# Another order for the first loads of a fused attention and two-layer gated network

## The chip, the core and the metric

The kernel runs on one core of a Trainium2 chip. The metric is device time in microseconds (us) for one execution of the whole program, as the median of several runs on one chip. The engines are named as the profile names them: PE (TensorE, matmul), PEld (its weight load), DVE (VectorE), ACT (ScalarE), POOL (GpSimd) and SP (SyncE, which here issues all the loads and stores).

## The reference

Windowed causal attention with a linear bias by distance, over 4 batches, 8 heads, 576 positions and 64 dimensions, feeds two feed-forward layers over 2304 tokens of width 512. All data are float32.

```python
scores = q @ k.T / sqrt(D) + bias            # window of 128 positions, causal
attn = softmax(scores);  x = attn @ v        # x: 2304 x 512
x = (silu(x @ w_gate) * (x @ w_val)) @ moe_w_out       # d_ff 1536
h = x @ moe2_w_in
y = (h * tanh(softplus(h))) @ moe2_w_out               # d_ff 2048
```

## The kernel before, in words

The weights come in as 64-bit floats, so each block of 1 MB is loaded raw and converted on the core into 32-bit numbers, and these are split into a high and a low half for the products. Converting one block takes one ACT instruction (line 420), five on DVE (lines 435, 440, 425, 428 and 446), and then one ACT instruction (line 121, the high half) and one on DVE (line 124, the low half).

The tokens are cut into five chunks (512, 384, 512, 512 and 384). The attention of the first chunk stands alone at the start of the kernel. After it, the first layer of chunk c is interleaved on PE with the attention of chunk c+1; the second layer comes last. In the first chunk the eight heads go in four pairs. The loads of pair r are called q_r, k_r and v_r here: q and k are one load of 256 KB each and hold both heads of the pair, v is four loads of 64 KB. A head passes through S (scores on PE, line 114; mask and row minimum on DVE, lines 221, 228 and 235; exponential on ACT, line 239; norm on DVE, lines 247 and 250, then on ACT and POOL, lines 254 and 256), T (transposes on PE, line 261; copy on ACT, line 267; two masks on POOL, lines 270 and 274) and, for each pair, O (product with v on PE, then the halves of xt on ACT and DVE, lines 121 and 124). `split` (line 185) scales the q of a pair once on ACT before its first scores.

The order of the first loads is written out in `first()`: for each pair its q, k and v, with weight block w0 (tile wst) after the third pair. After the first score piece come o0, the first block of the output weights (tile wraw), then w1, w2 and w3. The raw blocks share a pool of 12 buffers with the four pairs' tiles and the converted blocks. `conv_w1` and `conv_ring` put the steps of a conversion into a list `bg`, and a loop over the attention's 28 pieces (score, transpose and output pieces of the first chunk) takes steps from it at a rate set by `conv_a` and `conv_b`.

Only PE keeps the order in which the program is written. On the other engines, and on the queue of SP, a planner settles the order when the kernel is built, from the dependencies, the order of the program and its own estimates of cost. At run time each engine takes its instructions in that fixed order, and an instruction that waits holds up all that stand behind it.

Of the kernel before, what the change touches and what calls it, by code (L numbers as in the profile page):

```python
# [18 lines left out]
B, H, S, D = 4, 8, 576, 64  # L19
# [11 lines left out]

SLOT = {1: 0, 2: 1, 3: 2, 5: 3, 6: 4, 7: 5, 4: 6}
CFG = dict(
    order="SSOT", delay0=2, early=[4], pbufs=10, pump_g=2, pump_p=2, lag=4, lastlag=6, evprio=500,
    conv_a=0.1, conv_b=0.9,
)


# [54 lines left out]
def body(ctx: ExitStack, tc: tile.TileContext, qT, kT, vP, w1, w1o, w2, cst, yT):  # L93
# [41 lines left out]
    def attention(ap, p, ci, s_native, upfront):  # L135
# [5 lines left out]
        def s_full(h):  # L141
            return h // 2 < s_native

        def load(h):
            pr, e = divmod(h, 2)
            if s_full(h) and e:
                return
            if upfront:
                t = wp.tile([128, 2048], F32, tag="w", name="qkv")
                q, k = t[:, :p.n], t[:, 512:512 + p.nk]  # L150
                raw["v", pr] = t[:, 1152:1152 + 128 * len(p.kb)].rearrange("p (k d) -> p k d", d=128)
            elif s_full(h):
                q = ap.tile([128, p.n], F32, tag=("qraw", "Q")[pr % 2], name="q32")
                k = ap.tile([128, p.nk], F32, tag=("K1", "KL")[pr % 2], name="k32")
            else:
                q = ap.tile([128, p.n], F32, tag="qraw", name="qraw")
                k = ap.tile([128, p.nk], F32, tag="kraw", name="kraw")
            for s in p.segs:
                cq, ck = slice(s.c0, s.c0 + s.n), slice(s.koff, s.koff + s.kn0 + s.n)
                sq, sk = slice(s.s0, s.s0 + s.n), slice(s.s0 - s.kn0, s.s0 + s.n)  # L160
                if s_full(h):
                    nc.sync.dma_start(out=q[:, cq], in_=qT[s.b, h:h + 2, :, sq].rearrange("h d s -> (h d) s"))
                    nc.sync.dma_start(out=k[:, ck], in_=kT[s.b, h:h + 2, :, sk].rearrange("h d s -> (h d) s"))
                    continue
                for e in range(2):
                    nc.sync.dma_start(out=q[64 * e:64 * e + 64, cq], in_=qT[s.b, h, :, sq])
                    nc.sync.dma_start(out=k[64 * e:64 * e + 64, ck], in_=kT[s.b, h, :, sk])
            raw[h] = (q, k)
            if upfront:
                load_v(pr)  # L170

        def load_v(pr):
            if ("v", pr) not in raw:
                raw["v", pr] = ap.tile([128, len(p.kb), 128], F32, tag=f"v{pr % 2}", name="v")
            v = raw["v", pr]
            for x in p.kb:
                for r in range(128 // x.n):
                    nc.sync.dma_start(out=v[r * x.n:(r + 1) * x.n, x.vi, :], in_=vP[x.b, pr, x.k0:x.k0 + x.n, :])
# [122 lines left out]
    early = {}  # L301

    def attention_pieces(atts):

        heads = [(a, h) for a in atts for h in range(H)]
        pairs = [(a, r) for a in atts for r in range(HP)]
        n = len(heads)
        out = []

        def run(k, f):  # L310
            a, h = heads[k]
            return getattr(a, f)(h)

        def load(k):
            if not heads[k][0].upfront:
                run(k, "load")

        def load_v(r):
            if not pairs[r][0].upfront:
                pairs[r][0].load_v(pairs[r][1])  # L320

        def first():
            if atts[0].upfront:
                for h in range(0, H, 2):
                    run(h, "load")
                    for f in early.pop(h, []):
                        f()
            load(0)
            load_v(0)
            run(0, "split")  # L330
            load(1)
            load_v(1)

        def s_piece(k, g):
            a, h = heads[k]

            def f():
                if k == 0 and g == 0:
                    first()
                a.score(h, g)  # L340
                if g == a.ns - 1:
                    a.norm(h)
                    if k + 1 < n:
                        run(k + 1, "split")
                        if k + 2 < n:
                            load(k + 2)

            return (a.ci, 1.7 if a.s_full(h) else 0.87, f)

        def o_piece(k):  # L350
            a, h = heads[k]

            def f():
                if a.ci not in x_t:
                    x_t[a.ci] = xp.tile([128, 2, CT, 512], F32R, tag="x", name="xt")
                a.outp(h // 2)
                r = a.ci * HP + h // 2 + 2
                if r < len(pairs):
                    load_v(r)

            return (a.ci, a.nk * 0.46, f)

        def t_piece(k):
            a, h = heads[k]
            return (a.ci, 0.48, lambda: a.transp(h))

        def delay(k):
            return CFG["delay0"] if heads[k][0].ci == 0 else 1

        for st in range(n + 4):  # L370
            todo = {"S": [], "T": [], "O": []}
            if st < n:
                todo["S"] = [s_piece(st, g) for g in range(heads[st][0].ns)]
            for k in range(max(0, st - 4), min(st, n)):
                if k + delay(k) == st:
                    todo["T"].append(t_piece(k))
                if k + delay(k) + 1 == st and heads[k][1] % 2 == 1:
                    todo["O"].append(o_piece(k))
            for c in CFG["order"]:
                if todo[c]:  # L380
                    out.append(todo[c].pop(0))
            for c in "SOT":
                out += todo[c]
        out.sort(key=lambda x: x[0] > 0)
        return out
# [8 lines left out]
    def pump(n):  # L394
        while n > 0 and bg:
            k, f = bg.popleft()
            f()
            n -= 1
            if k is not None:
                done.add(k)  # L400
# [70 lines left out]
    def stage_w1(i):  # L471
        stage[i] = wp.tile([128, 2048], I32, tag="w", name="wst")
        nc.sync.dma_start(out=stage[i], in_=w1[i].bitcast(I32))

    def stage_other(key, src):
        stage[key] = bpool["a"].tile([128, 2048], I32, tag="wraw", name="wraw", bufs=1)
        nc.sync.dma_start(out=stage[key], in_=src.bitcast(I32))

    def conv_w1(i):
        st = {}  # L480

        def put(w):
            wt[i] = w
            stage.pop(i)
            if i + 4 < NF1:
                stage_w1(i + 4)

        steps(("w", i), convert(stage[i], st) + halves(st, w_tile, put))

    def conv_ring(r):  # L490
        st = {}

        def spill_it():
            nc.sync.dma_start(out=w1od[r], in_=st["w"])

        def put(w):
            ring[0, r] = w
            stage.pop(("o", r))
            if r + 1 < NF1 // 2:
                stage_other(("o", r + 1), w1o[r + 1])  # L500

        steps(
            ("ring", 0, r),
            convert(stage["o", r], st) + [spill_it] + halves(st, ring_tile, put),
        )
# [411 lines left out]
    with tc.manual_schedule(engines={mybir.EngineType.PE}):  # L917
# [18 lines left out]
        atts = [attention(app, p, ci, S_FULL[ci], ci == 0) for ci, p in enumerate(plansA)]  # L936
# [1 line left out]
        lasts = [max(j for j, x in enumerate(pieces) if x[0] == ci) + 1 for ci in range(len(plansA))]  # L938
        at = 0
        stages = [lambda: stage_w1(0), lambda: stage_other(("o", 0), w1o[0]), lambda: stage_w1(1)]  # L940
        for h, k in zip(CFG["early"], range(3)):
            early.setdefault(h, []).append(stages[k])
        stages = stages[len(CFG["early"]):]
        while at < lasts[0]:
            pieces.popleft()[2]()
            at += 1
            if at == 1:
                for f in stages:
                    f()
                conv_w1(0)  # L950
                conv_ring(0)
                conv_w1(1)
                nst = len(bg)
                stage_w1(2)
                stage_w1(3)
            f = (at / lasts[0] - CFG["conv_a"]) / (CFG["conv_b"] - CFG["conv_a"])
            while bg and nst - len(bg) < f * nst:
                pump(1)
        carry = []
        for ci, p in enumerate(plansA):  # L960
# [11 lines left out]
            if 1 <= ci < last:  # L972
                k = last - 1
                for i in range((ci - 1) * NF2 // k, ci * NF2 // k):
                    conv_w2(i)
            lag = CFG["lastlag"] if ci == last else 1
# [36 lines left out]
        for f in carry:  # L1013
# [5 lines left out]
        load = nc.scalar.add_instruction(  # L1019
            mybir.InstLoadActFuncSet(name=nc.get_next_instruction_name(), act_func_set_id=25)  # L1020
        )
# [62 lines left out]
```

## Time and profile before

| | |
|---|---|
| median of 3 runs | 969.74 us (969.54 to 971.17) |
| the profiled execution | 970.98 us, of which span 968.9 us |
| PE busy | 929.1 us (96%) |
| PEld busy | 829.6 us (86%) |
| DVE busy | 718.1 us (74%) |
| ACT busy | 526.9 us (54%) |
| POOL busy | 218.8 us (23%) |
| loads and stores | 174.86 MB, mean 180 GB/s |

The span is the time from the first to the last instruction, and all times in the trace count from its start. Busy shares are means over the whole span: the stretch that the change touches is the first 64 us, in which the shares are others than these.

### The profile page before, as it was taken

Reading aid. Unit: us, or ns where it says so; the run is one execution under the profiler, and the core shown is the slowest. Engines: PE = TensorE matmul, PEld = TensorE weight load, DVE = VectorE, ACT = ScalarE, POOL = GpSimd, SP = SyncE. Lnnn points to the kernel's source line nnn. Section 1 sums busy time; section 2 is a strip of 40 time slices with the busy share of each in tenths; the row PEclk is TensorE's granted clock in tenths of the full one; section 3 lists DMA queues with packets and bytes.
Section 4 is the critical chain, followed back from the end, with each engine's and each line's share of the span. In section 5 each row is a group of like instructions: output and inputs, shape, how many; then the busy total and the mean of one; then the engine's idle time right before and its main releaser. Section 6 shows DMA issues by size and latency. Waiting matters only on the chain. (4 is left out here: it accounts for less than half of the span.)

```text
span 968.9 us, 14644 instructions
## 1 busy us (share of the span) xinstructions
PE 929.1 (96%) x5040; PEld 829.6 (86%) x5040; DVE 718.1 (74%) x1359; ACT 526.9 (54%) x1135; POOL 218.8 (23%) x348
## 2 busy tenths in 40 slices
PE   7789999999999999999998998899999999999998
PEld 5447777898998888887877998889999999999997
DVE  5999999788768865478534768778886788777673
ACT  6856667666666664455433445455544645454442
POOL 2531234211110322001014233552012320122000
PEclk9889999999999999999999999999999999999999
DMA  8763334476546743176306993624784257830385
GB/s 285 261 252 143 119 133 148 139 236 220 170 130 195 249 130 115 31 243 216 118 1 221 387 329 106 232 83 145 256 298 148 66 173 251 312 114 21 96 264 183
DMA packets 76921, 174.86 MB, mean 180 GB/s; under 512 B 9136, under 2 KB 52528, under 8 KB 67120
## 3 DMA queue, kind: packets, MB, share of 16 engines
q1 hardware_dynamic: 76848, 173.94, 54.1%
q8 instruction: 40, 0.66, 0.3%
q14 instruction: 33, 0.27, 0.1%
HBM read 138.25 MB, written 35.65 MB: 179 GB/s over the span
## 5 line engine op out<-in xcount | busy, mean ns | idle before, releaser
L114 PE MATMUL g_ps<-xt,w 128*128 128x512 f32 (+1 forms) x1440 | 316.3, 373 | 1.2 <-DVE xt L124 1.2
L114 PEld LDWEIGHTS g_ps<-xt,w 128*128 128x128 f32 x1440 | 258.1, 188 | 37.7 <-issue 2.0
L114 PE MATMUL bk<-xs,win 128*128 128x384 f32 x1008 | 179.0, 336 | 8.1 <-DVE G L684 6.0
L114 PEld LDWEIGHTS bk<-xs,win 128*128 128x128 f32 x1008 | 174.4, 188 | 12.2 <-DVE G L684 9.7
L114 PE MATMUL bk<-op,wout 128*128 128x384 f32 x1008 | 175.8, 334 | 0.8 <-DMA wout<-w2o 0.7
L114 PEld LDWEIGHTS bk<-op,wout 128*128 128x128 f32 x1008 | 174.8, 188 | 1.4 <-issue 1.4
L114 PE MATMUL acc<-hh,ring 128*128 128x512 f32 (+1 forms) x480 | 148.9, 373 | 1.6 <-DVE ring L124 1.5
L121 ACT ACTIVATE op<-G 128x768 fp32r<-128x768 f32 x84 | 70.7, 846 | 66.0 <-PE bk L114 63.4
L114 PEld LDWEIGHTS acc<-hh,ring 128*128 128x128 f32 x480 | 89.0, 188 | 14.9 <-DVE ring L124 2.3
L124 DVE TENSOR_TENSOR op<-G,op 128x768 fp32r<-128x768 f32 x84 | 80.2, 962 | 27.2 <-ACT op L121 26.7
L270 POOL TENSOR_SCALAR_AFFINE_SELECT PT<-PT 128x256 f32<-128x256 f32 (+4 forms) x80 | 42.6, 546 | 253.4 <-ACT PT L267 253.2
L780 POOL TENSOR_TENSOR t<-w 128x256 f32<-128x256 f32 x48 | 44.4, 945 | 224.3 <-DVE win L124 207.7
L114 PE MATMUL acc<-hl,ring 128*128 128x512 f32 (+1 forms) x240 | 88.5, 369 | 1.7 <-DVE hl L124 1.7
L239 ACT ACTIVATE Pt<-Pt,sm 128x128 f32<-128x128 f32 (+1 forms) x160 | 62.5, 392 | 21.5 <-DVE sm L235 21.2
L619 DVE SCALAR_TENSOR_TENSOR t<-t,g_ps 128x512 f32<-128x512 f32 (+1 forms) x60 | 37.6, 627 | 37.4 <-ACT t L618 37.2
L684 DVE TENSOR_TENSOR G<-u,bk 128x384 f32<-128x384 f32 x72 | 38.9, 552 | 31.3 <-PE bk L114 29.2
L1028 ACT ACTIVATE G<-G 128x384 f32<-128x384 f32 x72 | 36.9, 520 | 44.2 <-DVE G L684 44.2
L618 ACT ACTIVATE t<-g_ps 128x512 f32<-128x512 f32 (+1 forms) x60 | 32.8, 547 | 50.3 <-PE g_ps L114 50.2
L627 DVE SCALAR_TENSOR_TENSOR t<-t,g_ps 128x512 f32<-128x512 f32 (+1 forms) x60 | 37.8, 631 | 27.1 <-PE g_ps L114 26.4
L121 ACT ACTIVATE hh<-t 128x512 fp32r<-128x512 f32 (+1 forms) x60 | 35.0, 583 | 41.4 <-DVE t L627 41.4
L254 ACT ACTIVATE Pt<-Pt,sm 128x128 f32<-128x128 f32 (+1 forms) x144 | 46.3, 390 | 12.9 <-DVE sm L250 12.8
L274 POOL TENSOR_SCALAR_AFFINE_SELECT PT<-PT 128x256 f32<-128x256 f32 (+4 forms) x80 | 52.9, 678 | 1.6
(79 smaller groups left out, 1282.2 us busy)
## 6 DMA issues: line engine op xcount, KB each, us to landing
wout<-w2o SPq DMA_DIRECT2D x42, 1024.0 KB, 5.6
wraw<-w SPq DMA_DIRECT2D x16, 1024.0 KB, 5.3
w2o<-chl SPq DMA_DIRECT2D x16, 896.0 KB, 8.6
wst<-w SPq DMA_DIRECT2D x12, 1024.0 KB, 7.2
cw<-w1od SPq DMA_DIRECT2D x24, 512.0 KB, 4.0
w<-w2d SPq DMA_DIRECT2D x24, 512.0 KB, 3.4
w2d<-cw SPq DMA_DIRECT2D x16, 512.0 KB, 4.0
wraw<-w1o SPq DMA_DIRECT2D x6, 1024.0 KB, 6.4
```

Of the source, the lines that this page charges most:

```text
L114: nc.tensor.matmul(out=out, lhsT=lhsT, rhs=rhs, start=start, stop=stop, skip_group_check=True)
L121: return nc.scalar.activation(out=out, in_=in_, func=AF.Copy)
L124: return nc.vector.tensor_tensor(out=out, in0=in_, in1=hi.bitcast(F32), op=ALU.subtract)
L239: nc.scalar.activation(out=Pt[:q.qn], in_=Pt[:q.qn], func=AF.Exp, scale=-1.0, bias=sm[:q.qn, i:i + 1], accum_out=sm[:q.qn, 8 + i:9 + i],)
L254: nc.scalar.activation(out=pt, in_=pt, func=AF.Copy, scale=r)
L270: nc.gpsimd.affine_select(out=here, in_=prev, pattern=[[0, m], [1, n]], compare_op=ALU.is_ge, fill=0.0, base=0, channel_multiplier=-1,)
L274: nc.gpsimd.affine_select(out=prev, in_=prev, pattern=[[0, m], [-1, n]], compare_op=ALU.is_gt, fill=0.0, base=0, channel_multiplier=1,)
L619: nc.vector.scalar_tensor_tensor(out=t[:, :n], in0=t[:, :n], scalar=1.0, in1=st["g"][:, :n], op0=ALU.add, op1=ALU.mult)
L627: nc.vector.scalar_tensor_tensor(out=t[:, :n], in0=t[:, :n], scalar=0.5, in1=vps[:, :n], op0=ALU.mult, op1=ALU.mult)
L684: nc.vector.tensor_tensor(out=out, in0=a, in1=b, op=op)
L780: nc.gpsimd.tensor_tensor(out=x[:, o], in0=a, in1=b, op=ALU.subtract)
L1028: nc.scalar.activation(out=out, in_=in_, func=AF.Mish)
```

## The change

The order of the first loads becomes a list, in which q stands for a pair's q and k, v for its values, and w0, w1, w2 for the three first stages (block w0, then o0, then block w1). `load` no longer loads the values itself. All three stages are now issued in `first()`, and `conv_a` falls from 0.1 to 0.0: the first step of a conversion is offered after the first piece of the attention (before: after the third); the last of the 22 steps is offered after piece 26 in both.

Order before: q0 k0 v0, q1 k1 v1, q2 k2 v2, w0, q3 k3 v3, o0, w1, w2, w3. Order after: q0 k0, w0, q1 k1, v0, q2 k2, o0, v1, q3 k3, v2, w1, v3, w2, w3.

```diff
-    order="SSOT", delay0=2, early=[4], pbufs=10, pump_g=2, pump_p=2, lag=4, lastlag=6, evprio=500,
-    conv_a=0.1, conv_b=0.9,
+    order="SSOT", delay0=2, early=["q0", "w0", "q1", "v0", "q2", "w1", "v1", "q3", "v2", "w2", "v3"], pbufs=10, pump_g=2, pump_p=2, lag=4, lastlag=6, evprio=500,
+    conv_a=0.0, conv_b=0.9,
...
             raw[h] = (q, k)
-            if upfront:
-                load_v(pr)
...
             if atts[0].upfront:
-                for h in range(0, H, 2):
-                    run(h, "load")
-                    for f in early.pop(h, []):
-                        f()
+                for c, i in ((x[0], int(x[1])) for x in CFG["early"]):
+                    {"q": lambda: run(2 * i, "load"), "v": lambda: atts[0].load_v(i), "w": lambda: early[i]()}[c]()
...
         stages = [lambda: stage_w1(0), lambda: stage_other(("o", 0), w1o[0]), lambda: stage_w1(1)]
-        for h, k in zip(CFG["early"], range(3)):
-            early.setdefault(h, []).append(stages[k])
-        stages = stages[len(CFG["early"]):]
+        early.update(enumerate(stages))
...
             if at == 1:
-                for f in stages:
-                    f()
                 conv_w1(0)
                 conv_ring(0)
                 conv_w1(1)
```

## Rows read from the trace of the kernel before

**Rows 1.** Busy time by stretch: busy us of each engine, PE clock, DMA share, GB/s.
```profile
8.33:17.14 8.81, 8.81 (x31) 7.14 (x31) 5.27 (x34) 6.77 (x26) 1.65 (x6) 1.00 0.95 306
17.14:29.80 12.66, 10.42 (x35) 5.95 (x33) 12.62 (x31) 10.10 (x26) 6.12 (x7) 1.00 0.99 370
...
43.06:64.15 21.09, 13.07 (x51) 6.90 (x51) 19.01 (x36) 14.31 (x30) 9.25 (x13) 0.76 0.89 327
64.15:129.35 65.20, 63.81 (x295) 47.36 (x295) 59.98 (x133) 39.91 (x99) 12.69 (x22) 1.00 0.37 129
```

**Rows 2.** Waits of PE, 6 to 64.2: us, times, longest.
```profile
PE o_ps L114 <- POOL PT L274: 6.6, 5, 3.0
...
PE t_ps L261 <- POOL Pt L256: 1.4, 3, 1.0
```

**Rows 3.** Timeline of PE: start us, duration us; idle time before it in brackets.
```profile
6.22 7.10 PE L114 MATMUL s_ps<-qkv 64*128 64x256 f32 x24 [6.22 <-ACT qkv L185]
...
64.15 0.72 PE L114 MATMUL g_ps<-xt,w 128*128 128x512 f32 x2 [1.24 <-DVE xt L124]
```

**Rows 4.** Waits of DVE, 8.33 to 17.3: us, times, longest.
```profile
DVE sm L247 <- ACT Pt L239: 2.1, 2, 1.3
DVE cw L435 <- DMA wst<-w: 0.9, 1, 0.9
```

**Rows 5.** Timeline of the queue of SP: start of an issue, its duration.
```profile
4.08 0.43 SPq L162 DMA_DIRECT2D qkv<-qT  x1
...
8.48 1.91 SPq L178 DMA_DIRECT2D qkv<-vP  x4
10.43 0.43 SPq L473 DMA_DIRECT2D wst<-w  x1
10.90 0.43 SPq L162 DMA_DIRECT2D qkv<-qT  x1
...
14.33 0.65 SPq L477 DMA_DIRECT2D wraw<-w1o  x1
17.14 1.67 SPq L473 DMA_DIRECT2D wst<-w  x3
```

**Rows 6.** Loads of rows 5, in their order from q1, us from issue to landing.
```profile
qkv<-qT SPq DMA_DIRECT2D x1, 256.0 KB, 4.4
...
wst<-w SPq DMA_DIRECT2D x1, 1024.0 KB, 6.7
qkv<-qT SPq DMA_DIRECT2D x1, 256.0 KB, 6.9
...
wraw<-w1o SPq DMA_DIRECT2D x1, 1024.0 KB, 7.9
...
wst<-w SPq DMA_DIRECT2D x1, 1024.0 KB, 7.6
```

**Rows 7.** Timeline of DVE: the six instructions that convert block w0.
```profile
17.14 0.69 DVE L435 TENSOR_SCALAR cw<-wst 128x1024 int32<-128x1024 int32 x1 [0.87 <-DMA wst<-w]
17.87 1.23 DVE L440 SCALAR_TENSOR_TENSOR cw<-wst,cw 128x1024 f32<-128x1024 uint32 x1
...
19.01 0.42 DVE L425 TENSOR_SCALAR cp<-cg 128x512 int32<-128x512 int32 x1
...
19.86 0.68 DVE L428 SCALAR_TENSOR_TENSOR cp<-cg,cp 128x512 int32<-128x512 int32 x1
...
21.14 1.31 DVE L446 SCALAR_TENSOR_TENSOR cw<-cw,cp 128x1024 f32<-128x1024 f32 x1
...
26.36 1.21 DVE L124 TENSOR_TENSOR w<-cw,w 128x1024 fp32r<-128x1024 f32 x1
```

**Rows 8.** Timeline of ACT: q1's scale, head 0's first exponential, w0's first step.
```profile
8.48 0.72 ACT L185 ACTIVATE qkv<-qkv,cst_sb 128x512 f32<-128x512 f32 x1 [2.31 <-DMA qkv<-qT]
9.19 0.40 ACT L239 ACTIVATE Pt<-Pt,sm 128x128 f32<-128x128 f32 x1
...
17.14 1.16 ACT L420 ACTIVATE cg<-wst 128x1024 bf16<-128x1024 bf16 x1 [0.64 <-DMA wst<-w]
```

## The prediction

> **What bounds the kernel now.** I read the busy time by stretches first, because the change touches only the start. From 64.15 us on PE is the bound: of the 65.20 us up to 129.35 it is busy 63.81 [rows 1]. So whatever moves the moment at which PE gets the last part of the first chunk's xt moves the end, as long as DVE keeps up; DVE is busy 59.98 of the same 65.20 us and has 5.2 us to spare. That moment is 64.15 us, where PE goes on after 1.24 us of waiting for the low half of xt from DVE [rows 3].
>
> Then I asked what sets the 64 us. The waits of PE between 6 and 64 us name POOL: 6.6 us for the masks of PT, 1.4 us for the norm on POOL [rows 2]. But POOL has work for only 9.25 of the last 21.09 us of that phase, so it is not its own load that sets the time [rows 1]. The stretches show who is full: between 17.14 and 29.80 us DVE is busy 12.62 of 12.66 us, and between 43.06 and 64.15 us 19.01 of 21.09 [rows 1]. In both stretches DVE alternates between attention and the conversion of weights. The reader is to see the contrast with the stretch before: from 8.33 us (its first score) to 17.14 us DVE is busy 5.27 of 8.81 us, so 3.54 us lie idle [rows 1]. It waits there 2.1 us for exponentials and, at the end, 0.9 us for block w0 to land [rows 4]. At 17.14 us w0 lands, and its conversion begins on ACT and DVE in the same instant [rows 7, 8].
>
> **How the loads queue.** The first of v2 is issued at 8.48 us, which is when q1 lands (4.08 plus 4.4), and w1 is issued at 17.14 us, when w0 lands (10.43 plus 6.7) [rows 5, 6]. Between the members of each couple stand seven other loads. So in this program a load is issued only when the one eight places before it has landed. With that and about 0.47 us for an issue (10.43 to 10.90) [rows 5] the new order can be counted through.
>
> **The change, part by part.** *w0 goes forward.* It is the fourth load; four issues before q1's old place (4.08) give about 2.2 us. With its own 6.7 us it lands at 8.9 us. The row had a longer queue ahead of it, so that may be late; with the slowest load of a block among these, 7.9 us [rows 6], it is 10.1. So it comes about 8 us earlier, into the stretch in which DVE has idle time. Its six DVE instructions are 0.69 + 1.23 + 0.42 + 0.68 + 1.31 + 1.21 = 5.54 us [rows 7]. The idle time is 3.54 us. Lower bound of the gain: only the wait for w0 itself goes, 0.9 us [rows 4]. Upper bound: all 3.54 us are filled. I take two thirds, 2.4 us: the pieces are about as long as the longest gap (1.3 us) [rows 4], so a piece put into a gap will often stick out and delay an instruction of the attention, but there are several gaps and w0 is there before most of them.
>
> *ACT.* Two instructions of w0 move with it, 1.16 us [rows 8] and a high half that I take as the same. ACT is idle 8.81 - 6.77 = 2.04 us in that stretch [rows 1], so they just fit: 0, and up to 1.2 us lost if one of them stands before exponentials that are due.
>
> *q1 and k1 go behind w0.* q3 was issued directly behind w0 and took 6.9 us, against q1's 4.4 [rows 6]. Issued at 2.67 us, q1 lands at 9.57 instead of 8.48, and its scale of 0.72 us [rows 8] ends at 10.3. PE needs it for the third of three heads, whose 24 matmuls take 7.10 us from 6.22 [rows 3]: two thirds of it end at 10.95. So PE still has work for 0.6 us and this costs 0. Without that cover it costs the 1.1 us by which q1 is later.
>
> The Trainium skill speaks against this edit: by "DMA: Bandwidth & Descriptors", section "Queues, rings and completion order", each DMA engine consumes descriptors in the order of its ring, so that q1 would wait for the whole of w0. At the 306 GB/s of the stretch [rows 1] the 1.05 MB of w0 are 3.4 us instead of the 2.5 us by which q3 was slower; q1's scale would end at 11.2, PE would wait 0.3 us, and the sum below would be -2.1 instead of -2.4. No run here shows the rings themselves.
>
> *Values go back.* v0 is issued from 3.6 to 5.5 us and so lands by about 10; O comes after the scores of three heads, whose matmuls end at 13.3 us [rows 3], and v1 is needed two heads later still. Nothing waits: 0.
>
> *o0, w1, w2, w3.* k2 must wait for w0 (8.9), o0 for q1 (9.57). o0 lands at 9.57 + 7.9 = 17.5 instead of 22.2. The second load of v2 stands eight places behind o0 and so waits until 17.5; w1, three issues later, goes at about 18.9, 1.8 us later than now, and w2 and w3 with it. w1 lands then at 26.5 instead of 24.7 us. DVE has o0 to convert until then, as full as it is from 17.14 to 29.80 [rows 1], so 0; if it ran dry, up to 1.8 us. The next chunk's loads behind these move by as much; PE reads them only after 64 us.
>
> *First steps offered at once.* The steps are offered two pieces earlier, but none can run before w0 lands at 8.9 us. 0 by itself; it lets the planner use the gaps that the first term counts.
>
> **Sum.** -2.4 + 0 + 0 + 0 = -2.4 us. The profiled execution took 970.98 us (span 968.9 and 2.1 around it), so 968.6; that execution was 1.24 us above the median of the runs, so against the median it is 967.3 us. About 0.2%, or 1.9 us, can be told from no change. Bounds of the first term alone: 966.2 to 968.8.
>
> **The rivals.** *Given back.* DVE is full from 17.14 us on because the planner fills it with conversions that PE does not need yet. If w0 leaves this stretch, later blocks may take its place, and the chain through POOL at 43 to 64 us stays as long as it is. For it: PE idles 8.0 of 21.09 us there [rows 1], and POOL's masks are its longest wait [rows 2]. Against it: later blocks can't come earlier than their loads, and w1 to w3 land later, not earlier. Time 969.7.
>
> *More than that.* The granted PE clock in 43.06 to 64.15 us is a mean of 0.76 [rows 1], a mix of 2.4 and 1.2 GHz, in a stretch in which PE is idle for 8.0 us. If the waits go, PE's 13.07 us become 9.9 at full clock: up to 3.1 us more. For it: after 64.15 us, where PE hardly idles, the mean is 1.00 [rows 1]. Against it: the waits of this stretch are not removed by the change itself. Time 964.2.
>
> *Slower: ACT is held up at the start.* The scale of q1 stands ahead of head 0's first exponential on ACT now, and waited 2.31 us for its load [rows 8]. If the planner keeps it there and puts w0's first step ahead of both, ACT stands until w0 has landed. With a landing at 10.1 us: 1.16 to 11.3, 0.72 to 12.0, and the exponentials begin at 12.0 instead of 9.19. Every head follows: +2.8 us, and DVE, which waits for the exponentials, has the same idle time as before. Time 972.5. It decides from a landing of about 9.7 us on, where the delay exceeds what DVE gains. For it: the planner's estimate was too early each time here (2.31 us at q1, 0.64 us at w0 [rows 8]). Against it: with q1 behind 1 MB its own estimate moves too.
>
> **How the numbers follow.** The gain by filling idle time has 0.46, of which 0.08 lies under 1.9 us; more than that 0.08; given back 0.28; slower 0.18, of which 0.01 is too small to be told. Faster: 0.38 + 0.08 = 0.46. Same: 0.08 + 0.28 + 0.01 = 0.37. Slower: 0.17. The range reaches from the clock's case to near the held-up ACT: 964.0 to 971.8. The likeliest case by itself holds 966.2 to 968.8.
>
> **What the profile after would show.** Right: the first step on wst near 9 us, DVE busy over 7 us between 8.3 and 17.1, the issue of w1 near 19 us, q1's scale from about 9.6 us, and the row where PE goes on after the last xt at about 61.8 us. Wrong: head 0's first exponential later than 10 us on ACT (held up); that last row at 64 us in spite of the early w0 (given back); or an unlike order of the conversions on DVE further on, which would move PE's waits after 64 us by amounts that none of the terms contains.

## The result and the profile after

The changed kernel takes 975.58 us (974.8 to 978.77, 5 runs) against 969.74 us before (967.27 to 971.93, 5 runs). The ratio is 1.0069, 95% interval 1.0047 to 1.0092: slower by 0.7%, or 5.8 us between the medians. The profiled execution took 974.84 us, its span 972.9 us against 968.9, so a comparison of the two traces has to explain 4.0 us. Line numbers in the conversions and the attention are 2 to 4 lower than before.

The stretches that answer to [rows 1]; the columns are the same.

```profile
8.33:17.14 8.81, 7.92 (x26) 6.33 (x25) 7.60 (x30) 5.91 (x20) 0.88 (x3) 1.00 1.02 358
17.14:29.80 12.66, 10.46 (x31) 6.84 (x31) 12.66 (x35) 10.29 (x30) 7.93 (x11) 1.00 0.98 360
29.80:43.06 13.26, 12.34 (x64) 8.44 (x60) 12.10 (x45) 11.45 (x35) 6.31 (x13) 1.00 0.71 231
43.06:64.15 21.09, 12.11 (x46) 6.16 (x47) 19.03 (x32) 13.35 (x29) 11.75 (x14) 0.61 0.82 299
64.15:129.35 65.20, 64.75 (x297) 48.06 (x296) 59.99 (x127) 38.14 (x91) 9.98 (x22) 1.00 0.40 137
```

DVE (third of the engines) is busy 7.60 us where it was busy 5.27: the hole is filled, as foretold. But in the next stretch it is as full as it was, 12.66 of 12.66 us, and between 43.06 and 64.15 us it is busy 19.03 us where it was 19.01. Nothing has been taken out of the later stretches. For the stretch from 29.80 us, which [rows 1] leaves out, the kernel before has:

```profile
29.80:43.06 13.26, 12.55 (x53) 8.49 (x52) 11.83 (x40) 10.80 (x31) 10.97 (x15) 0.74 0.65 220
```

What the loads did, in the queue of SP (start of an issue, its duration), answering to [rows 5]:

```profile
2.18 0.43 SPq L469 DMA_DIRECT2D wst<-w  x1
2.65 0.43 SPq L162 DMA_DIRECT2D qkv<-qT  x1
...
9.76 0.33 SPq L163 DMA_DIRECT2D qkv<-kT  x1
10.44 0.33 SPq L473 DMA_DIRECT2D wraw<-w1o  x1
...
17.23 0.43 SPq L469 DMA_DIRECT2D wst<-w  x1
...
23.76 0.36 SPq L473 DMA_DIRECT2D wraw<-w1o  x1
```

and the times from issue to landing, answering to [rows 6], of w0, q1 and o0 in turn:

```profile
wst<-w SPq DMA_DIRECT2D x1, 1024.0 KB, 7.6
...
qkv<-qT SPq DMA_DIRECT2D x1, 256.0 KB, 7.8
...
wraw<-w1o SPq DMA_DIRECT2D x1, 1024.0 KB, 5.5
```

w0 lands at 2.18 + 7.6 = 9.78 us, and k2, eight places behind it, is issued in that moment (9.76). q1 lands at 10.45. The last row is the load of o1, the second block of the output weights. In the kernel before it was issued 10 us later (queue of SP):

```profile
33.87 0.35 SPq L477 DMA_DIRECT2D wraw<-w1o  x1
```

The timeline of ACT, answering to [rows 8], is the first row that went another way:

```profile
5.44 0.72 ACT L183 ACTIVATE qkv<-qkv,cst_sb 128x512 f32<-128x512 f32 x1
9.76 1.13 ACT L416 ACTIVATE cg<-wst 128x1024 bf16<-128x1024 bf16 x1 [3.60 <-DMA wst<-w]
10.80 0.39 ACT L237 ACTIVATE Pt<-Pt,sm 128x128 f32<-128x128 f32 x1
...
11.57 0.70 ACT L183 ACTIVATE qkv<-qkv,cst_sb 128x512 f32<-128x512 f32 x1
```

From 6.16 to 9.76 us ACT does nothing. It waits for w0, whose first step stands ahead of head 0's exponentials; these start at 10.80 instead of 9.19 us. Most of the 3.60 us cost nothing, as there was nothing to do: PE waited for k0 and began its scores 1.2 us later than before, and DVE had the first row minimum only at 10.26 us (timeline of DVE):

```profile
10.18 0.08 DVE L233 DVE_READ_ACCUMULATOR2_ANT sm<- 128x1 f32 x1
```

So of the 1.6 us about 0.5 are due to the place of w0's step. PE shows what follows (its timeline; compare [rows 3]):

```profile
7.42 8.26 PE L114 MATMUL s_ps<-qkv 64*128 64x256 f32 x24 [7.42 <-DMA qkv<-kT]
...
32.98 2.25 PE L114 MATMUL s_ps<-qkv 64*128 64x256 f32 x8
...
40.75 1.78 PE L114 MATMUL s_ps<-qkv 64*128 64x256 f32 x8
...
58.39 1.11 PE L114 MATMUL o_ps<-PT,qkv 128*64 128x256 f32 x2 [4.00 <-POOL PT L272]
...
66.85 0.73 PE L114 MATMUL g_ps<-xt,w 128*128 128x512 f32 x2 [0.45 <-DVE xt L124]
```

PE goes on behind the last xt of the first chunk at 66.85 us, where it was 64.15. The four low halves of that chunk's xt end at 33.6, 46.5, 56.8 and 66.8 us, against 31.1, 43.7, 54.5 and 64.1 before: later by 2.5, 2.9, 2.3 and 2.7. So in this pair of executions the first xt is already as late as the last. The waits of PE between 6 and 64 us, answering to [rows 2], with one for k0's load, and one for ACT that came to 1.0 us before:

```profile
PE o_ps L114 <- POOL PT L272: 7.7, 5, 4.0
PE s_ps L114 <- DMA qkv<-kT: 7.4, 1, 7.4
PE t_ps L259 <- ACT Pt L252: 3.0, 3, 1.5
```

w0's six DVE instructions did move into the hole (timeline of DVE; the first two rows are the first and the sixth of those in [rows 7]), and between its first score and 17.3 us DVE has no wait any more, where [rows 4] had two groups:

```profile
10.39 0.69 DVE L431 TENSOR_SCALAR cw<-wst 128x1024 int32<-128x1024 int32 x1
...
20.69 1.24 DVE L124 TENSOR_TENSOR w<-cw,w 128x1024 fp32r<-128x1024 f32 x1
...
55.52 0.69 DVE L431 TENSOR_SCALAR cw<-wst 128x1024 int32<-128x1024 int32 x1 [1.76 <-DMA w1od<-cw]
56.13 0.68 DVE L124 TENSOR_TENSOR xt<-o_ps,xt 128x512 fp32r<-128x512 f32 x1
...
57.76 3.21 DVE L436 SCALAR_TENSOR_TENSOR cw<-wst,cw 128x1024 f32<-128x1024 uint32 x2
...
66.12 0.68 DVE L124 TENSOR_TENSOR xt<-o_ps,xt 128x512 fp32r<-128x512 f32 x1
```

The last rows show what took their place: up to the last xt DVE runs one conversion behind another. At 55.52 us one of them stands 1.76 us for the store of a buffer that it is to overwrite, with an xt queued behind it. (Before, the like wait of 2.08 us stood behind that xt, at 56.57 us.) Counted over the whole stretch, 42 conversion instructions (40.6 us) stand ahead of the last xt on DVE, where there were 37 (35.0 us). Beside the two of line 436 POOL's masks are slow (timeline of POOL):

```profile
55.99 1.30 POOL L268 TENSOR_SCALAR_AFFINE_SELECT PT<-PT 128x512 f32<-128x512 f32 x2 [1.83 <-ACT PT L265]
57.25 2.65 POOL L272 TENSOR_SCALAR_AFFINE_SELECT PT<-PT 128x512 f32<-128x512 f32 x2
```

The two masks of line 272 take 2.65 us here; in the kernel before the same two took 0.63 and 0.64 us, at a moment when DVE waited.

### The profile page after: what moved, and what is told of

It reads as the page before. It is cut to its first block, busy times and chain, and to the rows that moved or that the text cites. A ratio compares the mean times of both kernels' runs of the same rounds, so it can differ in the third digit from the quotient of the medians.

```text
span 972.9 us, 14634 instructions
## 1 busy us (share of the span) xinstructions
PE 928.3 (95%) x5040; PEld 829.7 (85%) x5040; DVE 717.5 (74%) x1359; ACT 525.1 (54%) x1135; POOL 205.0 (21%) x348
## 4 chain that ended last, share of the span: by engine, by line
PE 71%; DVE 11%; DMA 9%; ACT 3%; issue 3%; POOL 2%; SPq 1%; DVEq 0%; ACTq 0%; POOLq 0%
PE bk L114 31%; PE g_ps L114 24%; PE acc L114 11%; PE s_ps L114 3%; DMA wraw<-w 3%; PE o_ps L114 2%; DMA w2d<-cw 2%; DMA w<-w2d 1%; DVE cw L436 1%; DVE cw L442 1%; PE t_ps L259 1%; POOL t L776 1%; DVE G L680 1%; DMA x2d<-ev 1%; DMA w1od<-cw 1%
## 5 line engine op out<-in xcount | busy, mean ns | idle before, releaser
L268 POOL TENSOR_SCALAR_AFFINE_SELECT PT<-PT 128x256 f32<-128x256 f32 (+4 forms) x80 | 40.5, 521 | 233.3 <-ACT PT L265 233.1
L124 DVE TENSOR_TENSOR hl<-t,hh 128x512 fp32r<-128x512 f32 (+1 forms) x60 | 40.7, 679 | 15.1 <-ACT hh L121 14.6
```

The source lines that it names most:

```text
L124: return nc.vector.tensor_tensor(out=out, in0=in_, in1=hi.bitcast(F32), op=ALU.subtract)
L268: nc.gpsimd.affine_select(out=here, in_=prev, pattern=[[0, m], [1, n]], compare_op=ALU.is_ge, fill=0.0, base=0, channel_multiplier=-1,)
```

## The experiments

Four theories, by the names that the expectations use. **START:** the loss is made in the first 20 us; w0 shares the transfers with the first k and q, and its first step on ACT stands ahead of head 0's exponentials. **END:** it is made at the end of the first chunk; o2's first step on ACT stands ahead of the last copies of PT, and POOL's last masks run beside conversions. **LATE:** the order on ACT and DVE from about the fifth chunk on, of which the kernels here show two, is the worse one. **BUDGET:** early loads let the planner place more conversions ahead of the last xt of the first chunk.

The 18 kernels were each timed in 5 rounds against the kernel before. The columns from the third on come from the profiled execution alone. How far it scatters is seen from e8, which has the order of the kernel before: by 2.0 us in the last xt and by 3.5 us in the span. The columns are: first exponential on ACT; conversion instructions on DVE ahead of the last xt; end of that xt; issue of the first store of x2d, the first results of the phase behind the attention; span.

| run | ratio to before, 95% | exp | conv. | last xt | x2d | span |
|---|---|---|---|---|---|---|
| before | 1 | 9.19 | 37 | 64.1 | 195.3 | 968.9 |
| changed | 1.0069 [1.0047, 1.0092] | 10.80 | 42 | 66.8 | 197.8 | 972.9 |
| e1_a_tail | 1.0047 [1.0021, 1.0073] | 10.83 | 41 | 68.5 | 200.7 | 979.9 |
| e2_a_start | 1.0026 [1.0006, 1.0046] | 9.25 | 40 | 62.9 | 195.1 | 971.0 |
| e3_q0q1w0 | 1.0067 [1.0042, 1.0091] | 9.29 | 43 | 67.7 | 200.7 | 976.8 |
| e4_w0_only | 1.0082 [1.0054, 1.0109] | 11.19 | 40 | 68.0 | 200.4 | 972.8 |
| e5_v_only | 1.0043 [1.0027, 1.0058] | 9.51 | 40 | 65.2 | 198.5 | 971.1 |
| e6_start_tail | 1.0019 [1.0001, 1.0036] | 9.38 | 40 | 64.1 | 195.3 | 967.2 |
| e7_q0q1w0_tail | 1.0049 [1.0035, 1.0064] | 9.97 | 42 | 66.5 | 199.8 | 973.0 |
| e8_conva0 | 0.9995 [0.9977, 1.0013] | 9.60 | 37 | 62.1 | 193.7 | 965.4 |
| e9_a_hold4 | 1.0008 [0.9994, 1.0022] | 10.50 | 36 | 62.7 | 192.8 | 965.7 |
| e10_a_hold | 1.0033 [1.0016, 1.0050] | 10.63 | 30 | 59.7 | 195.7 | 967.9 |
| e11_b_hold | 1.0031 [1.0016, 1.0046] | 9.18 | 30 | 60.9 | 198.4 | 973.5 |
| e12_q_hold | 1.0016 [0.9999, 1.0033] | 9.21 | 30 | 63.4 | 197.0 | 970.8 |
| e13_start_hold4 | 1.0006 [0.9990, 1.0023] | 9.26 | 36 | 61.6 | 192.9 | 964.2 |
| e14_q_hold4 | 1.0074 [1.0050, 1.0098] | 9.67 | 36 | 65.7 | 201.0 | 974.8 |
| e15_v_hold4 | 1.0044 [1.0026, 1.0062] | 9.64 | 35 | 64.2 | 199.6 | 974.7 |
| e16_b_hold4 | 0.9972 [0.9957, 0.9988] | 9.92 | 35 | 62.3 | 194.1 | 968.5 |
| e17_loads_early | 1.0046 [1.0029, 1.0062] | 9.78 | 37 | 65.6 | 198.8 | 973.1 |
| e18_loads_early_hold4 | 1.0040 [1.0020, 1.0060] | 9.45 | 35 | 66.3 | 198.5 | 971.7 |

What the table tells as a whole: from the first store of x2d to the end the 20 executions need 771.3 to 779.2 us, 773.9 in the mean, while the store itself lies between 192.8 and 201.0. The two, store and span, go together with a correlation of 0.91. With the ratios of the medians the time of the store goes together with 0.85, and the time behind it with 0.27. So most of what tells these kernels apart happens in the first 200 us.

### The second edit, and the two ends of the stretch

**e8_conva0** is the kernel before with the second edit only:

```diff
-    conv_a=0.1, conv_b=0.9,
+    conv_a=0.0, conv_b=0.9,
```

> The kernel before with conv_a 0.0 alone. No theory gives it a price: the first steps can't run before w0 lands at 17.1 us, so the order on every engine should stay. Ratio 1.000 within 0.2%, last xt at 64.1 us.

Measured: 969.25 us, no difference. Its instructions stand in the same order as before on every engine. The changed kernel, too, has the same order on every engine whether `conv_a` is 0.0 or 0.1. So the second edit does nothing, and the loss comes from the order of the loads.

**e1_a_tail** is the changed kernel with o2's first step on ACT behind the last copy of PT of the first chunk (`copies[0]`):

```diff
+            def held():
+                with tc.issue_after(copies[0].ins):
+                    first_step()
+            fs[0] = held
```

> The changed kernel; only on ACT, the first step of block o2 is held behind the last copy of PT of the first chunk (in the changed kernel it stands before the last two copies and waits for its load). Theory END (what the start loses is made up by 41 us, and the loss that counts arises at 54 to 60 us, where the last two copies stand behind o2's step and POOL's masks then run beside DVE's conversions): the last xt comes at about 64 instead of 66.85 us, the time falls by 2 to 3 us. Theory START (the loss is the late k0 and the late exponentials of head 0, and passes through): last xt stays at 66.9 us, time as the changed kernel within 1 us.

Measured: 974.15 us. About 2 us of the loss went, which is inside the intervals of the two. By the medians END is a third of it, and it is not told from nothing.

**e2_a_start** is the changed kernel with w0's first step on ACT behind head 0's exponentials, with the same few lines and `exps[0, 0]` in the place of `copies[0]` (`conv_a` is 0.1 here and in e4 to e6, e13, e15, e17 and e18; as said, the changed kernel's order is the same with both values).

> The changed kernel; only on ACT, the first step of w0 is held behind the exponentials of head 0 (in the changed kernel it stands before them and ACT waits 3.6 us for w0 to land). START: the first exponential comes at about 10.4 instead of 10.8 us and T of head 1 at 20 instead of 22.5 us, and the end comes 1.5 to 3 us earlier. END: the start gets faster as said, but o2's step still stands before the last copy, so last xt stays near 66.9 us and the time within 1 us of the changed kernel.

Measured: 972.84 us, so 0.43% less than the changed kernel (1.0026 against 1.0069). ACT no longer waits for w0 (its waits up to 17.3 us hold no line for wst):

```profile
ACT L184 <- DMA qkv<-qT: 4.2, 1, 4.2
ACT Pt L238 <- DVE sm L234: 3.9, 2, 3.0
ACT qkv L184 <- DMA qkv<-qT: 0.3, 1, 0.3
```

The wait for DVE is the one for the first scores, and head 0's exponentials begin at 9.25 us. By the medians the edit takes back 4 us of the 6 to 7; by the two intervals it may be 1 to 7. That is more than the 0.5 to 1.6 us by which the exponentials were late. With w0's step the planner also moved other work: 40 conversion instructions stand ahead of the last xt instead of 42. So this run prices the edit with all that moved, and not the late exponentials alone.

**e6_start_tail** has both edits.

> The changed kernel with both holds: w0's first step behind head 0's exponentials and o2's first step behind the last copy of PT. END: the same as the hold at the end alone within 1 us, last xt near 64 us. START: better than either hold alone by 1.5 us or more. LATE: from the last xt to the end 906 us, so 971 us, not 969.7.

Measured: 972.03 us; END adds 0.7 us to e2, less than can be told.

### Other orders of the loads

In e3 the list has the second pair's q and k ahead of w0; e4 brings w0 forward and leaves values where they were; e5 puts values behind the next pair's q and k and leaves w0 near its old place:

```diff
e3: "q0 q1 w0 v0 q2 w1 v1 q3 v2 w2 v3"
e4: "q0 w0 v0 q1 v1 q2 v2 q3 v3 w1 w2"
e5: "q0 q1 v0 q2 v1 w0 q3 v2 w1 v3 w2"
```

> The changed kernel with w0 one place further back in the list, behind q1 and k1, all else the same. k0 no longer shares the DMA engines with w0, and the planner puts w0's first step behind head 0's exponentials. START: first scores at 6.2 us as before the change, first exponential at about 9.2, all of the loss gone: 969 to 971 us. END: the start is as before the change, but o2's first step stands before the last two copies of PT on ACT, as in the changed kernel: last xt 66 to 67 us, 973 to 976 us.

> The order before the change with w0 alone moved forward, to directly behind k0; the values stay with their pairs, o0 and w1 behind all pairs. The start has the same fault as the changed kernel (k0 shares with w0, w0's first step before head 0's exponentials on ACT), but at the end of the attention o2's step stands behind both copies of PT, and the order from the fourth chunk on is that of the kernel before. START: as slow as the changed kernel, 973 to 976 us. END: last xt at 63 to 65 us, 968 to 971 us.

> The changed list with w0 back behind v1 (q0 q1 v0 q2 v1 w0 q3 v2 o0 and so on): only the values go behind the next pair's q and k. The start is as before or better, o2's first step stands behind both last copies of PT, the order from the fourth chunk on is that of the changed kernel. START and END: last xt at 62 to 64 us. Theory LATE (the order of DVE and ACT from the fourth chunk on, which the planner chose otherwise in the changed kernel, costs 1 to 2 us at 600 to 720 us): from the last xt to the end 906 us as in the changed kernel, not 904.7 as before the change; time 969 to 970 us. Without LATE 967 to 969 us.

Measured: 977.28, 978.09 and 974.33 us. e4 has the worst start (exponentials at 11.19 us, ACT waits 3.96 us for w0) and the worst time. But e3 has a clean start, 9.29 us, and is no better than the changed kernel. A late start can't be the only cost. e5 costs 0.43% with w0's first step on ACT at 14.19 us.

**e7_q0q1w0_tail** is e3 with e1's edit.

> w0 behind q1 and k1, and o2's first step held behind the last copy of PT; here the order from the fourth chunk on is that of the kernel before. END: last xt at 62 to 64 us, as good as the kernel before or better: 968 to 970 us. LATE: from the last xt to the end 904.7 us as in the kernel before. START: no better than the same list without the hold.

Measured: 974.36 us, 0.18% less than e3; again some 2 us for END, not resolved from none.

**LATE** falls by the traces of e1 to e8. The order of before on DVE and ACT from the fifth chunk on stands also in e4, e7 and e8, the other order in the changed kernel and in e1, e2, e3, e5 and e6. But from the last store of x2d to the end the former group needs 360.4 to 361.4 us and the latter 360.6 to 362.1, and e4, with the order of before, is the slowest of all. So LATE can hold a fraction of a microsecond, and not the loss.

### Conversions held back

**e9_a_hold4** is the changed kernel with all conversions of the weight blocks from the fifth and the o blocks from the third held, on ACT and DVE, behind the last xt of the first chunk. Nothing else is edited, and up to about 50 us the order on ACT and DVE is that of the changed kernel:

```diff
+    def behind(fs, wait):
+        def held(f):
+            def g():
+                with tc.issue_after(last_xt[0][0].ins), tc.issue_after(last_xt[0][1].ins):
+                    f()
+            return g
+        return [held(f) for f in fs] if wait else fs
...
-        steps(("w", i), convert(stage[i], st) + halves(st, w_tile, put))
+        steps(("w", i), behind(convert(stage[i], st) + halves(st, w_tile, put), i >= 4))
```

(and the same for the o blocks with `r >= 2`). **e10_a_hold** holds from the fourth weight block on, **e11_b_hold** does that to the kernel before, **e12_q_hold** to e3.

> The changed kernel; on ACT and DVE the conversions of w4 and later and of o2 and later are held behind the last xt of the first chunk. So 36 DVE instructions of conversions stand before that xt instead of 42; before the change there are 37. Theory BUDGET (DVE is full from 17 us to the last xt, and each instruction of a conversion that the planner puts ahead of it beyond those of the kernel before makes it later by about its 1 us): most of the loss goes, 969 to 972 us, last xt at 62 to 64.5 us. START (the loss comes from the late k0 and head 0's late exponentials): 973 to 976 us.

> The changed kernel; the conversions of w3 and later and of o2 and later are held behind the last xt of the first chunk: 30 DVE instructions of conversions ahead of it. BUDGET: last xt at 58 to 62 us; whether the end comes as much earlier depends on DVE, which has 5 us to spare in the 65 us after it and gets 12 us more to do there: 966 to 970 us. START: last xt not before 64 us, 971 us or more.

> The kernel before with the same hold (w3 and later, o2 and later behind the last xt of the first chunk): 30 instead of 37 DVE instructions ahead of it. BUDGET: last xt at 57 to 61 instead of 62 to 64 us; the end up to 3 us earlier, 966 to 969 us, less if PE then waits for w3. If the conversions ahead of the last xt cost nothing, as START has it, 969.5 us and last xt at 62 to 64.

> The list with w0 behind q1 and k1, with the hold of w3 and later and o2 and later: 30 DVE instructions of conversions ahead of the last xt instead of 43. BUDGET: as the changed kernel with that hold or 1 to 2 us better, since k0 and head 0's exponentials are not late here. START: as the same list without the hold, 975 to 977 us.

Measured: 970.51, 972.49, 972.77 and 970.68 us. In e9 nearly the whole loss is gone although ACT still waits for w0 (timelines of ACT and PE):

```profile
9.45 1.15 ACT L416 ACTIVATE cg<-wst 128x1024 bf16<-128x1024 bf16 x1 [3.25 <-DMA wst<-w]
...
10.50 0.39 ACT L238 ACTIVATE Pt<-Pt,sm 128x128 f32<-128x128 f32 x1
```

```profile
62.74 0.73 PE L114 MATMUL g_ps<-xt,w 128*128 128x512 f32 x2 [0.67 <-DVE xt L124]
```

Head 0's exponentials start 1.3 us later than before, and the first two xt end late as well (32.6 and 45.5 us). Yet PE goes on behind the last xt at 62.74 us, no later than before (64.15, and e8 has its last xt at 62.1). Between the third xt and the last three conversion instructions stand on DVE, where the changed kernel has nine and the kernel before eight. So nearly the whole loss can be taken back behind 50 us, with the start as it is. e12 shows that a hold can help the list of e3 too (0.5% back), and e10 that a stronger hold is worse than e9's. e11 shows the limit: with 30 ahead the first chunk ends 1 to 3 us earlier (against e8 and against the profile before) and the kernel is slower, because the work is owed behind it. PE waits for DVE in the second chunk's attention (waits of PE between 58 and 200 us; before, the same line says 2.3 us in 2 times):

```profile
PE s_ps L114 <- DVE Q L196: 5.4, 2, 3.6
```

### Is it a sum of two?

**e13_start_hold4** has e2's edit and e9's; **e14** is e3 with e9's hold, **e15** e5 with it, and **e16** the kernel before with it.

> The changed kernel with both suspected costs taken away: the first step of the first weight block stands behind head 0's exponentials on ScalarE, and the conversions of the weight blocks from the fifth and of the o blocks from the third stand behind the last xt of the first chunk (36 conversion instructions on VectorE ahead of that xt, as in the run that held them and left the start alone). BUDGET alone: the same as that run, 970.5 us, ratio 1.000 to 1.002. START adds its own 1 to 4 us: 966.5 to 969.5 us, ratio 0.996 to 0.999, first exponential near 9.25 us. Neither: over 972 us.

> The second pair's q and k ahead of the first weight block (clean start: k of the first pair alone in the queue) and the same hold, 36 conversion instructions ahead of the last xt. Without the hold this order of loads took 977.3 us with 43 of them ahead, with a stronger hold (30 or fewer) 970.7. BUDGET: 969 to 971 us. If the loads' order itself costs something besides: 972 us or more. START: 966.5 to 969.5 us.

> Values behind the next pair's q and k, the first weight block only behind the third pair's, and the same hold, 35 conversion instructions ahead of the last xt. Without the hold this order took 974.3 us with 40 of them ahead. BUDGET: 969 to 971 us, level with the kernel before. If what the later values delay is a cost of its own: 972 us or more.

> The kernel before with the same hold: 35 conversion instructions ahead of the last xt in the place of 37, loads as before. BUDGET with its best place near 36: no change, 969 to 970.5 us, ratio 0.998 to 1.001. If each conversion ahead of that xt costs its own duration: 968 us. If holding itself costs (the work is owed behind the xt at once, as in the run with 30 ahead, 972.8 us): 971 us or more.

Measured: 970.49, 977.07, 974.13 and 966.58 us. e13 equals e9: with the hold, mending the start is worth nothing that can be told, so START and BUDGET don't add up. e14 and e15 equal e3 and e5: this hold is worth nothing there, at the same number ahead. So BUDGET as a count is refuted; 35 or 36 conversions ahead go with anything from 0.9972 to 1.0074. In e14 DVE even stands idle for 2.82 us ahead of the last xt, so there it isn't DVE's queue that makes it late:

```profile
65.01 0.69 DVE L124 TENSOR_TENSOR xt<-o_ps,xt 128x512 fp32r<-128x512 f32 x1 [2.82 <-ACT xt L121]
```

And e16 beats both kernels: 0.9972, interval 0.9957 to 0.9988. Of the kernel before's waits of DVE between 30 and 65 us, 2.1 us for a store and 1.1 us for o1, neither is left (waits of DVE in e16):

```profile
DVE xt L124 <- ACT xt L121: 1.0, 1, 1.0
DVE w L124 <- ACT w L121: 0.2, 1, 0.2
```

Whether the 0.28% comes from these waits is not shown: the profiled execution of e16 was its slowest (970.24 us).

With the same hold the new order of the loads costs 1.0008 / 0.9972 = 0.36%, or 3.5 us, of the 0.69% that it costs without.

### The loads without the early conversions

**e17_loads_early** keeps the changed kernel's order of loads but lets the last 64 columns of w0, o0 and w1 come late, by small loads of their own (x0, x1, x2), so that no conversion can begin sooner than before. Three more loads are issued. **e18** adds e9's hold.

```diff
-    "q0 w0 q1 v0 q2 w1 v1 q3 v2 w2 v3"
+    "q0 w0 q1 v0 q2 w1 v1 q3 v2 x0 w2 v3 x1 x2"
...
+        cols = slice(0, 1984) if i < 2 else slice(0, 2048)
+        nc.sync.dma_start(out=stage[i][:, cols], in_=w1[i].bitcast(I32)[:, cols])
```

> The changed kernel's loads in their order, but of the first two weight blocks and the first o block the last 64 columns come by loads of their own (32 KB each, three loads more) at the end of the list, so that their conversions can't begin sooner than in the kernel before; 37 conversion instructions on VectorE stand ahead of the last xt of the first chunk, as in the kernel before. If the loss comes from the conversions that the early loads let in: level with the kernel before, 968.5 to 971 us. If it comes from the loads themselves (k of the first pair beside w0, values later): 973 us or more, as the changed kernel. Half of each: 971 to 973 us.

> The same with the conversions of the weight blocks from the fifth and of the o blocks from the third held behind the last xt of the first chunk (35 ahead). With that hold the loads of before took 966.6 us and the changed kernel's loads 970.5 us. Conversions' place: 966 to 968 us. Loads themselves: 970 us or more.

Measured: 974.06 and 972.82 us. The early conversions were taken away (one conversion instruction of 0.8 us on DVE between 10 and 20 us, against 8 in the changed kernel and 4 before), and two thirds of the loss are still there. The hold takes nothing off that can be told (e18, 1.0040). By the expectation that means "the loads themselves", but up to 65 us PE waits for no transfer, and the first two xt end at 30.2 and 40.5 us, earlier than before (31.1 and 43.7). The time goes between the second and the third, which ends at 55.9 (before: 54.5). ACT, DVE and PE in turn:

```profile
39.22 1.13 ACT L416 ACTIVATE cg<-wraw 128x1024 bf16<-128x1024 bf16 x1 [0.49 <-DMA wraw<-w1o]
40.25 1.14 ACT L416 ACTIVATE cg<-wst 128x1024 bf16<-128x1024 bf16 x1
...
42.63 1.06 ACT L121 ACTIVATE w<-cw 128x1024 fp32r<-128x1024 f32 x1
43.58 0.69 ACT L252 ACTIVATE Pt<-Pt,sm 128x128 f32<-128x128 f32 x2
```

```profile
44.10 0.69 DVE L431 TENSOR_SCALAR cw<-wraw 128x1024 int32<-128x1024 int32 x1 [1.75 <-DMA w1od<-cw]
```

```profile
44.04 1.19 PE L259 MATMUL t_ps<-cst_sb,Pt 128*128 128x128 f32 x4 [3.21 <-ACT Pt L252]
```

Three conversion steps (3.3 us) stand ahead of two normalizations of a head on ACT, for which PE waits 3.21 us, while DVE waits 1.75 us for the store of a conversion buffer. Before, PE's waits for that line came to 1.0 us between 30 and 65. So in this trace the loss goes through another interleaving of conversions and attention even though the conversions are late. What the three added loads cost by themselves, in the queue of SP, was not measured.

## Why the prediction was wrong

The forecast was 967.3 us, in 964.0 to 971.8; 975.58 us lies outside, on the slower side.

**The step that failed** is the first term, "-2.4 us" for DVE's idle time, together with the 0 for ACT. The mechanism up to the hole was right. w0's first DVE step came at 10.39 us, and DVE is busy 7.60 us in the stretch (over 7 was foretold). Wrong was that filled idle time is gained time. DVE is no less busy in the later stretches, since the planner placed five more conversion instructions (5.6 us) ahead of the last xt. The rival "given back" had this mechanism but priced it at nothing lost; here the xt that PE waits for was late as well. Against it the prediction held that later blocks can't come earlier than their loads. That is so, but a later load came earlier too: o1 was issued at 23.76 instead of 33.87 us, and its first DVE step ran at 38.38 instead of 42.04. That holding conversions back pays is shown for this order by e9 (0.6%) and for the order before by e16 (0.3%), and e11 and e14 show that it is no rule.

**ACT**, taken as 0 with 1.2 us at most, was not nothing. ACT stood 3.60 us for w0; what that delays is 0.5 us in the changed kernel's profile and 1.3 us in e9's, where the first scores were not late. Already by the prediction's own rows the two instructions do not "just fit": 2.32 us of work against 2.04 us of idle time. The rival "ACT is held up at the start" had a chance of 0.18. w0 landed at 9.78 us, just past the 9.7 from which it was to decide, and not at the 8.9 of the sum. One detail differed: q1's scale (11.57 us) stood behind the first two of head 0's four exponentials and not ahead of them, so that these began at 10.80 and not at 12.0. The rival's 972.5 us priced a delay of 2.8 us at the start and nothing further on.

**k0 beside w0** has no term in the sum. In the changed kernel's profile the scores begin at 7.42 us instead of 6.22, as PE waits for k0's load. Whether the order costs this is not shown: over the 20 executions the scores begin at 6.25 to 7.74 us with w0 directly behind k0, and at 6.21 to 7.01 us without.

**The queue** was right where it was counted: k2 was issued when w0 landed. w1 was issued at 17.23 and not at 18.9, since o0 took 5.5 us to land and not 7.9. q1 landed at 10.45 us, not 9.57. The Trainium skill, "DMA: Bandwidth & Descriptors", section "Queues, rings and completion order", says that each DMA engine consumes descriptors in ring order. The prediction's estimate by it, with q1 behind the whole of w0, was 0.9 us more, so about 10.5, and the trace's 10.45 agrees. PE did not wait for q1.

**Values back: 0** is not borne out as a part alone. e5 costs 0.43% with values and the later loads moved, though no matmul waits for values in its trace; which of its moves does it was not separated. **conv_a: 0** is right (e8). **The clock's rival** did not come: the granted clock between 43.06 and 64.15 us is 0.61 where it was 0.76, and from 29.80 to 43.06 us it is 1.00 where it was 0.74.

The last sentence of the prediction, "an unlike order of the conversions on DVE further on", named what would make it wrong, and gave it no chance. By e3 and e14, which have a clean start and lose as much as the changed kernel, what happens further on can make the whole loss.

**What stays open.** Mending the start (e2) and holding conversions (e9) each take back more than half, but together no more than the hold alone. Every kernel with another order of the loads is slower than the one before or level with it, whether its start is clean, its count is low or its conversions are late. That most of the difference arises in the first 200 us is shown by the stores of x2d. That the interleaving of conversions and attention there makes it is argued from the traces and not shown by a run. Which couple of instructions decides in each order was not settled. No kernel was run with the new loads and exactly the old order on ACT and DVE; e17 has the late conversions and their number, but not their places.

## What to carry to other kernels

When idle time on an in-order engine is to be filled with work from later, find out what the freed time is refilled with: if a planner fills it with more background work, the chain that the next stage waits for can get longer. A step that waits for a load should not stand ahead of work that is ready, on any of the engines that it uses. How much of the wait counts depends on when that work becomes ready: here 0.5 to 1.3 of some 3.5 us. Here it was worth more to hold background work behind the last result that the next stage needs (0.28% on the kernel before) than to bring its loads forward.

## What the runs showed of the hardware

Matmuls of one kind ran at two speeds, and this hides or shows a delay of microseconds. The changed kernel and e1 have the same order of instructions up to about 50 us and nearly the same start (exponentials from 10.80 and 10.83 us), and then the timeline of PE in e1 answers to the rows from 32.98 to 40.75 us of the changed kernel's above with:

```profile
33.01 3.35 PE L114 MATMUL s_ps<-qkv 64*128 64x256 f32 x8
...
44.67 1.78 PE L114 MATMUL s_ps<-qkv 64*128 64x256 f32 x8
```

The last of these groups is the same in both: e1 is 3.9 us later there. Eight score matmuls take 1.78 us at a granted clock of 1.00 (2.4 GHz), and 3.35 us where it is 0.50 (1.2 GHz), as in this stretch of the kernel before:

```profile
33.57:36.92 3.35, 3.35 (x11) 2.57 (x12) 3.35 (x14) 2.14 (x8) 3.17 (x6) 0.50 0.99 346
```

But in e1 the stretch of the slow group reads 1.00:

```profile
33.01:36.36 3.35, 3.35 (x10) 2.57 (x10) 2.23 (x3) 2.43 (x8) 1.27 (x3) 1.00 0.78 259
```

So the matmuls ran there at the pace of the lower level, and the column does not show why; the cause stays open. The 3.9 us are as much as the profiled pair differs in all, so a single pair of executions can't place a loss of this size; the medians have to.

POOL and DVE slow each other in some pairings. A mask of 128x512 took 0.63 us where DVE stood. From 57.25 us on in the changed kernel two masks took 1.3 us each and two conversion instructions of line 436 beside them 1.6 instead of 1.2. The two masks just before, beside conversion steps of line 431 and an xt, took 0.65 each.
